# One thousand positions of a hand-ordered issue sequence, in another order

## The chip, the core and the metric

The kernel runs on one core of a Trainium2 chip. A core has five instruction queues that matter here: TensorE (PE) for matrix products, VectorE (DVE), ScalarE (ACT) and GpSimd (POOL) for everything element by element, and SyncE (SP), which here only issues DMA transfers. Each engine takes its instructions strictly in the order in which the program issued them to it, and waits at an instruction whose inputs are not there. The metric is the device time of one execution in microseconds (us).

## What is computed

Two layers. The first is an attention over 4 batches, 8 heads, 768 positions and 64 channels per head: every query sees the keys less than 16 positions away, and beside them one summary per block of 32 positions (the maximum of the block's keys, the mean of its values). The second is a feed-forward layer on the 3072 rows of 512 that come out.

```python
scores_s = scale * np.einsum('bhsd,bhnd->bhsn', q, k_sum)
scores_s = scores_s + np.log(block)
scores_l_m = np.where(mask_l, scores_l, -1000000000.0)
...
h = x @ w_in
g = np.maximum(h, 0.0) + np.log1p(np.exp(-np.abs(h)))
return (g @ w_out).astype(np.float32)
```

## The kernel before, in words

The rows are cut into six x tiles of 512 rows (two chunks of 256), numbered 0 to 5. For each x tile there are four attention **units**: two chunks times two halves of the heads (hp 0 and hp 2). A unit is a chain across the engines: PE makes the scores (line 644), DVE masks them and takes the row maxima (L657), ACT takes the exponentials (L665), DVE inverts the sums (L672, L673), one of POOL, DVE or ACT normalises (L678, L681), the result is transposed (for x tile 0 by PE at L698 with a copy by ACT at L702; for the others by DVE at L711, a store to memory and four reloads, L719 and L723), and PE multiplies by the values (L742). Of this product x is kept as two parts, a rounded high half and a low half with the rest (x tile 0: ACT L772 and DVE L776; later tiles: a copy at L754, then L828 and L835).

The feed-forward layer of an x tile goes over 16 feature tiles in two phases of 8. For each feature tile PE makes a hidden product in two halves of 6 products (L1060; the first half reads the columns of x that hp 0 makes, the second those of hp 2), ACT takes the softplus twice (L1162 rounded, L1166 exact), DVE keeps the rest (L1170), and PE projects (L1177): eight products with the rounded part, four with the rest. For the first and last feature tile of a phase the projection is four tasks, one per 128 rows.

The weights arrive as 64-bit words and are turned into two parts by a chain that is spread over the engines: magnitude (L934 on DVE or L937 on ACT), clamp (L941), shift (L945), sign (L949), tail (L955 on ACT, L958 on DVE), the addition of the tail on POOL (L963), the high part (L967) and the low part (L974).

None of this is scheduled at run time. The kernel first declares 2071 **tasks**, numbered in the order of declaration, each a handful of instructions with one or more ways to run it (one way per engine that could). Then `Order.issue` walks through the string `SEQUENCE` and runs the tasks in its order: a bare number takes the first way, a letter a or b the second or third. So the sequence fixes the order of every engine's queue at once, SP's included; the position of a task relative to tasks of other engines does not matter, only the order among those of its own engine. Buffers are fixed by the declaration, with the number of copies that the kernel gives them: one for the scores of a unit, one for the q, k and v of a unit of later tiles, two of PSUM for hidden products.

The tasks of which the prediction speaks: 0, 1, 2 the constants (identity, ones, mask); 3 to 42 products that fill PE's time; 43 to 49 key loads with their maxima; 51 to 62 value rows, loaded by SP and summed by PE, and 63 ACT's mean of them (L442); 64 to 135 the four units of x tile 0 (66, 101, 102, 106 are loads of value windows, 73 the first mask, 76 the first normalisation, 88 the second exponential, 117 and 131 the values products of the last two units, 119, 121, 133 and 135 their low halves); 136 to 139 copies of the means into the value sums by SP (L448); 153 to 245 the weights of the first phase (167, 172, 181, 188, 197, 201, 204 by name below; 180 and 208 are loads); 246 to 305 the feed-forward of x tile 0 (246 and 247 the first hidden product, 255 and 256 the second, 262 the third, 251 the first projection, 299 the rounded softplus of the eighth feature tile, 302 to 305 its projections); 312 to 440 the units of x tile 1 (313 and 342 key copies, 319 a copy of key maxima, 351 a mask, 352 the exponential behind it, 395 scores, 406 and 434 the values products of the last two units, 410 a low half of the third unit); 373 a key maximum; 386, 387, 589 key copies; 441 and 442 the first hidden product of x tile 1; 569 scores and 608 a values product of x tile 2.

The code as it is issued:

Of the kernel before, what the change touches and what calls it, by code (L numbers as in the profile page):

```python
# [147 lines left out]
0 3 4 5 6 7 8 9 10 11 12 13 14 153 154 2 43 162 15 16 17 18 19 20 21 22 23 24 25 26 27 28 1 29 30 31 32 33 313a 163a  # L148
155 156 157 158 189 164 45 165 167a 68 166 168 190a 152 44 46 64 51 191 192 193 169 159 53 100 55 319 57 314b 160 47
49 72 73 171 52 194 54 59 61 74 86 34 104 195 161 180 48 196a 87 66 172a 50 35 105 56 58 60 62 75 88 76a 63 312 108  # L150
197 65 67 173 109 70 170a 174 77 122 181a 78 175 182 107 89 79 36 37 69 208 38 176a 123 39 71a 40 110 90 111 80 322 81
41 112a 124 91 101 198 102 341 136 82 92 93 94 84 95 323 209a 137 347 177 342a 199 96 340 183 178a 125 368 210 184 213
98 179 97 185 85 83 113 138 99 106 324 211 114 186 204a 325 326a 372 115 350 42 103 116 227 126b 117 187a 369 127 200a
129 212 327 201 217 128 130 386 351 131 120 118 188a 387b 134 132 352 119 328 121 133 139 135 228 373 214 353 246 202
370 146 371a 140 385 247 248 374 249 250 376 203 255 392a 229 256 257 329 395 251 378 205 258 315 317 321 330 259 354b
355 262 320 396 263 143a 316 215 380 332 232 206 207 375a 218 318 331 414b 269 230 149 264 270 252 253 254 265 377
141a 260 271 356 272 397 266 219a 261 333 381 273 382 398 413 343 357 346 420a 267 360 216 220 415a 221 334 276 399b
336 231 359 379 345 423 348 358 223 222 277 344 400 349 507 508b 283 284 233 512a 424 224 268 236 401 278 279 509b 280
285 286 515 361 237 425 287 234a 235 388 383a 426 533 384 147 534a 274 362 402 389 290 535b 538a 238a 405 391 225 403
# [5 lines left out]
550 549 448 529a 537 464 574 598 449 455 459 700a 460 684 465 466 456 462 575 467 693 599 461 552 468 562 708 688a 576  # L165
600 471 601 530a 727 691 553a 567 565 472 563 478 473 602 709 694 479 578 463 557a 564 726 531 728a 532a 474 480 481
475 482 555a 710 469 579 733 577 470 363 692a 711 568 736 755 756b 580 485 712a 581 151 603 754 486 476 713 759 604
605 477 590 585 606 595 586 596 558a 492 593 335 583a 487 493 488 737 591 738 489 494 528 739 483 584 592 495 607 762
# [1181 lines left out]
```

## Time and profile before

| | us |
|---|---|
| median of 3 runs (lowest to highest) | 623.44 (622.63 to 623.88) |
| the profiled execution, its own time | 623.92 |
| its span, first to last instruction | 622.1 |
| PE busy | 599.2 |
| DVE busy | 389.8 |
| ACT busy | 349.6 |
| POOL busy | 180.7 |

The span is what the trace covers; the time of an execution also holds 1.8 us around it. Busy times are unions of the instructions' spans, so an engine at 96% has hardly a hole. In a timeline each line is a run of equal instructions on one engine, with its start, its length and, in brackets, how long the engine sat idle before it and whose result it waited for.

### The profile page before, as it was taken

The numbers are of one execution on the slowest core, as the hardware profiler recorded it, in microseconds if no ns is written. First come the engines' busy times: TensorE is split into PE (matmuls) and PEld (weight loads), VectorE is DVE, ScalarE is ACT, GpSimd is POOL, SyncE is SP. The second block draws the span as 40 slices with busy tenths as digits, with TensorE's granted clock in tenths as the row PEclk, the third lists the DMA queues.
The fourth block names the chain that finished last, engine by engine and source line by source line (L and its number), as shares of the span: only waits on it lengthen the run. The fifth ranks groups of instructions, "written<-read, shape, count | busy, mean of one in ns | idle before, by whom it ended". The sixth has DMA issues, their size and how long they took to land.

```text
span 622.1 us, 12000 instructions
## 1 busy us (share of the span) xinstructions
PE 599.2 (96%) x4452; PEld 506.4 (81%) x4452; DVE 389.8 (63%) x1010; ACT 349.6 (56%) x859; POOL 180.7 (29%) x180
## 2 busy tenths in 40 slices
PE   7668999999999999999999999999999999999997
PEld 6457777887888888888888888889898988989996
DVE  5989998676356755444316579873665664564532
ACT  4899999869567677565436987442312322132211
POOL 5444354041323213121000754474410325003000
PEclk9989999999999999999999999999999999999999
DMA  8986776976758677567435630023050240030031
GB/s 296 323 273 191 225 243 216 278 211 222 260 173 256 208 229 236 186 185 239 122 108 178 222 142 1 1 90 114 1 170 1 101 136 1 33 103 1 31 106 67
DMA packets 66571, 96.12 MB, mean 155 GB/s; under 512 B 5873, under 2 KB 44625, under 8 KB 65745
## 3 DMA queue, kind: packets, MB, share of 16 engines
q1 hardware_dynamic: 66512, 95.36, 48.0%
q8 instruction: 35, 0.57, 0.4%
q14 instruction: 24, 0.19, 0.1%
HBM read 66.06 MB, written 27.26 MB: 150 GB/s over the span
## 4 chain that ended last, share of the span: by engine, by line
PE 83%; DVE 7%; ACT 4%; DMA 2%; SPq 2%; issue 1%; ACTq 0%; DVEq 0%
PE po L1177 38%; PE ph L1060 21%; PE hx L1100 9%; PE hy L1100 7%; PE xo L742 4%; PE sc L644 3%; DVE sp L657 1%; DMA raw<-w_out_dram 1%; DVE t L941 1%; DVE w L974 1%; ACT t L937 1%; ACT sp L681 1%; DVE ks L353 1%; DMA v<-vs 1%; SPq L723 1%
## 5 line engine op out<-in xcount | busy, mean ns | idle before, releaser
L1177 PE MATMUL po<-w,gh 128*128 128x512 f32 x768 | 203.2, 392 | 0.1
L1177 PEld LDWEIGHTS po<-w,gh 128*128 128x128 f32 x768 | 141.1, 188 | 29.7 <-DVE ob L1207 0.7
L1060 PE MATMUL ph<-xw,w 128*128 128x512 f32 x672 | 161.2, 391 | 1.0 <-DVE xw L776 1.0
L1060 PEld LDWEIGHTS ph<-xw,w 128*128 128x128 f32 x672 | 125.6, 188 | 28.2 <-DVE xw L776 1.4
L1177 PE MATMUL po<-w,gl 128*128 128x512 f32 x384 | 114.3, 391 | 0.0
L1177 PEld LDWEIGHTS po<-w,gl 128*128 128x128 f32 x384 | 70.9, 188 | 14.4 <-issue 0.3
L665 ACT ACTIVATE sp<-sp,nm 128x120 f32<-128x120 f32 x192 | 73.1, 385 | 4.9 <-DVE nm L657 4.7
L1162 ACT ACTIVATE gh<-hx 128x512 fp32r<-128x512 f32 x20 | 12.0, 600 | 107.3 <-DVE hx L1110 107.3
L963 POOL TENSOR_TENSOR t<-t,raw 128x1024 int32<-128x1024 int32 (+1 forms) x20 | 41.9, 2101 | 94.3 <-DVE t L949 66.0
L1170 DVE TENSOR_TENSOR gl<-ph,gh 128x512 fp32r<-128x512 f32 x56 | 38.1, 685 | 44.7 <-ACT ph L1166 44.6
L1162 ACT ACTIVATE gh<-ph 128x512 fp32r<-128x512 f32 x56 | 33.3, 597 | 46.0 <-PE ph L1060 45.7
L804 POOL TENSOR_TENSOR x<-r,x 128x512 fp32r<-128x512 f32 x23 | 30.1, 1319 | 68.6 <-DVE x L797 58.9
L657 DVE CUSTOM_DVE_ANT_0 sp<-sc,added 128x120 f32<-128x120 f32 x192 | 40.9, 277 | 4.2 <-PE sc L644 3.3
L665 ACT ACTIVATION_READ_ACCUMULATOR sp<-sp,nm 128x1 f32 x192 | 36.5, 190 | 0.0
L1100 PE MATMUL hx<-x,w 128*128 128x256 f32 x240 | 35.7, 285 | 0.0
L1100 PE MATMUL hx<-x,sw 128*128 128x256 f32 x240 | 35.5, 284 | 0.0
L1100 PEld LDWEIGHTS hx<-x,w 128*128 128x128 f32 x240 | 32.9, 190 | 2.1
L1100 PE MATMUL hy<-x,sw 128*128 128x256 f32 x240 | 34.4, 284 | 0.0
L1162 ACT ACT_TABLE_LOAD x23 | 29.5, 1283 | 8.5 <-PE ph L1060 8.1
L1166 ACT ACTIVATE ph<-ph 128x512 f32<-128x512 f32 x56 | 33.0, 591 | 0.0
L1100 PEld LDWEIGHTS hx<-x,sw 128*128 128x128 f32 x240 | 32.0, 190 | 0.8
L1100 PEld LDWEIGHTS hy<-x,sw 128*128 128x128 f32 x240 | 31.2, 191 | 0.2
(113 smaller groups left out, 835.6 us busy)
## 6 DMA issues: line engine op xcount, KB each, us to landing
squares<-tb SPq DMA_DIRECT2D x20, 512.0 KB
pT<-squares SPq DMA_DIRECT2D x80, 128.0 KB
raw<-w_out_dram SPq DMA_DIRECT2D x16, 512.0 KB
kf<-kT_dram SPq DMA_DIRECT2D x16, 384.0 KB
raw<-w_in_dram SPq DMA_DIRECT2D x6, 1024.0 KB
q<-qT_dram SPq DMA_DIRECT2D x20, 256.0 KB
raw<-r SPq DMA_DIRECT2D x20, 256.0 KB
part<-ob SPq DMA_DIRECT2D x10, 512.0 KB
```

Of the source, the lines that this page charges most:

```text
L644: nc.tensor.matmul(unit(g * NU + h * NPAIR + i)[r * QW:(r + 1) * QW, k0:k1], lhsT=q[rows, w * QW:(w + 1) * QW], rhs=k[rows], start=True, s ...
L657: nc.vector.tensor_tensor_reduce(out=sp()[:, n], in0=unit(n), in1=added()[:, kinds.index((lows[w], lows[w + 1]))], scale=-SCALE, scalar=FL ...
L665: nc.scalar.activation(sp()[:, n], sp()[:, n], AF.Exp, bias=nm()[:, n:n + 1], scale=-1.0, accum_out=ss()[:, n:n + 1],)
L742: nc.tensor.matmul(xo()[h * D:(h + 1) * D, g * CH + w * QW:g * CH + (w + 1) * QW], lhsT=tiles.v(g)[:, w, h * D:(h + 1) * D], rhs=queries(g ...
L804: engine.tensor_tensor(to(1), a(), to(0).bitcast(F32), op=ALU.subtract)
L963: nc.gpsimd.tensor_tensor(a, a, word(0, I32), op=ALU.add)
L1060: nc.tensor.matmul(ph(), lhsT=lhs(part, cc), rhs=xw[cc][0]()[:, xw[cc][1], a], start=cc == 0 and n == 0, stop=cc == NCC - 1 and n == 2,)
L1100: nc.tensor.matmul(to()[:, half], lhsT=lhs(wa, cc), rhs=of_x(xa)[:, cc * CH:(cc + 1) * CH], start=cc == 0 and m == 0, stop=cc == NG - 1 an ...
L1162: nc.scalar.activation(gh(), all_of(), AF.Softplus)
L1166: nc.scalar.activation(all_of(), all_of(), AF.Softplus)
L1170: nc.vector.tensor_sub(out=gl(), in0=all_of(), in1=gh().bitcast(F32))
L1177: nc.tensor.matmul(po[t](), lhsT=a()[:, t * P:(t + 1) * P], rhs=w2()[:, part, i2 * DM:(i2 + 1) * DM], start=f == f0 and i == 0, stop=f == ...
```

## The change

The first 1000 positions of `SEQUENCE` are issued in another order; position 1001 and all that follow are as they were. The tasks, their buffers and what they depend on are the same. Of the tasks in these positions 109 run on another of their engines (their letter changes): among the larger ones, the first normalisation (76) goes from DVE to POOL and nine others change too; two low parts of weights go from POOL to DVE and one (197) from DVE to POOL; of the value sums of later batches four go from DVE to POOL and three the other way; eight copies of finished rows go from DVE to ACT and one back; eleven high halves of x go from DVE to ACT and five back; key copies are dealt out anew. On ACT the table of the exponential and that of the softplus replace each other 50 times over the whole program instead of 46, the first load counted in.

Places in single queues, counted from 0 within the queue: SP loads the value rows 59 and 61 at places 12 and 13 (before: 15 and 16), copies 136 and 138 at 23 and 24 (29 and 34), window 66 at 25 (19), 208 at 26 (25), 180 at 27 (18), 101, 102 and 106 at 28, 32 and 33 (26, 28 and 35). The reloads of the first unit of x tile 1 (329 to 332) stand at 49 to 52 (45, 50, 57, 54). On PE, 246 and 255 come at 61 and 65, before and just after the values product 131 at 64 (before: 64 and 66, with 131 at 63); the projections 302 to 305 all stand ahead of values 434 (before: 302 ahead, the other three behind). On POOL, the mask constants (2) come before the identity (0), and copy 589 comes ahead of the low half 410 (before: behind it).

The first 17 of the 36 lines, before and after:

```diff
-0 3 4 5 6 7 8 9 10 11 12 13 14 153 154 2 43 162 15 16 17 18 19 20 21 22 23 24 25 26 27 28 1 29 30 31 32 33 313a 163a
-155 156 157 158 189 164 45 165 167a 68 166 168 190a 152 44 46 64 51 191 192 193 169 159 53 100 55 319 57 314b 160 47
-49 72 73 171 52 194 54 59 61 74 86 34 104 195 161 180 48 196a 87 66 172a 50 35 105 56 58 60 62 75 88 76a 63 312 108
-197 65 67 173 109 70 170a 174 77 122 181a 78 175 182 107 89 79 36 37 69 208 38 176a 123 39 71a 40 110 90 111 80 322 81
-41 112a 124 91 101 198 102 341 136 82 92 93 94 84 95 323 209a 137 347 177 342a 199 96 340 183 178a 125 368 210 184 213
-98 179 97 185 85 83 113 138 99 106 324 211 114 186 204a 325 326a 372 115 350 42 103 116 227 126b 117 187a 369 127 200a
-129 212 327 201 217 128 130 386 351 131 120 118 188a 387b 134 132 352 119 328 121 133 139 135 228 373 214 353 246 202
-370 146 371a 140 385 247 248 374 249 250 376 203 255 392a 229 256 257 329 395 251 378 205 258 315 317 321 330 259 354b
-355 262 320 396 263 143a 316 215 380 332 232 206 207 375a 218 318 331 414b 269 230 149 264 270 252 253 254 265 377
-141a 260 271 356 272 397 266 219a 261 333 381 273 382 398 413 343 357 346 420a 267 360 216 220 415a 221 334 276 399b
-336 231 359 379 345 423 348 358 223 222 277 344 400 349 507 508b 283 284 233 512a 424 224 268 236 401 278 279 509b 280
-285 286 515 361 237 425 287 234a 235 388 383a 426 533 384 147 534a 274 362 402 389 290 535b 538a 238a 405 391 225 403
-291 427a 226a 239 428 390 393 394 404 516 297 298 292 275 293 541 294 406 240 299 241 338a 429 142 687 144 242 243 281
-430 407a 282 300 517 560b 301 364a 244a 431 432 518 519b 245 366 433 411a 566a 561b 416 288 422 289 520 412a 542 417
-418 543 295 296 302 419 408 421 559 434 150 337 569 409a 521 410a 435a 367 439 365 304 305 437 339a 510 306a 511 522
-524 544 588b 309a 310a 440a 438a 545b 303 525 441 442 587 443 594a 546 450 514 523 570 589 444 451 145 452 513 453 597
-571 148 445 307a 526 681 547 685 527a 536 454 689 446 572 540 699 548 682 447 686 457 573a 705 551 683 690 458 698 539
...
+2 43 153 162 189 45 64 68 51 44 0 1 3 53 158 154 4 155 5 156 6 157 7 8 9 163a 159 10 11 12 164 160 13 165 167 14 166
+15 161 55 47 190a 16 17 168 18 19 313b 20 46 21 314b 22 23 57 24 191 25 26 192 72 319a 194 193 59 52 61 73 195 74 54
+100 86 49 196a 65 104 56 171 87 197a 88 69 105 58 70 60 312 62 75 169a 76 48 27 63 107 28 29 30 67 50 136 31 32 33 34
+35 138 103 108 89 170a 66 90 208 36 109 37 180 38 110 39 40 77 101 172 122 173 315 320 174 176a 152 79 123 71a 78 41
+80 42 124 81 175 111 322 112a 91 340 341 347 323 102 93 84 106 82 177 92 209a 83 85 342 94 178a 95 210 211 324 125 113
+368 372 198 199 115 350 385 181 114 182 212 96 179 183 116 227 117 318 184 213 98 325 326a 97 126b 99 246 214 327 369
+120 127 185 118 129 373 186 128 130 131 351 386 392a 187 255 132 370 134 376 328 140 352 133 137 119 135 121 247 200
+317 380 201 202 374 387 395 256 188 203 248 228 249 257 371 250 258 251 139 329 331 215 330 332 262 204 353 259 263
+229 354b 230 316 231 269 321 270 264 355 396 205 265 232 217 218 252 356 253 271 378 272 254 233 206 260 381 266 273
+207 397 333 216 261 343 345 276 349 234a 334a 414 219a 398 277 375 377 357 360 399b 358 413 283 420 220 221 346 348
+143a 284 223 400 359 267 344 401 222 382 278 279 236 268 415 285 280 224 286 423 287 361 424 425 274 402 237 388 390
+391 235 290 405 379a 275 403 389 507 383a 362 508b 509 291 384 393 394 297 225 226 426 427a 292 293 238a 404 298 336
+364 239 281 240 242 512a 241 515 294 365a 428 243 406 533 516 429 282 517 416 422 288 534 538a 418 419 535a 244a 245
+421 417 289 518 146 407 541 299 409 338a 411 430 519a 295 433 432 520 431 300 559 296 301 304 305 141 303 560a 561b
+566 681 149a 542 685 302 543 142 521 337a 434 412a 339a 569 435a 587 588a 589 594a 437a 306 366a 510 514 438 367 439
+307 440 410a 441 442 544 545 511 450 522 524 443 523 444 150 525 513 451 309 445 144 310 546 446 452 453 447 547 689
+448 683 682 449 147 148 455 686 454 570 571 526 597 527a 531a 536 548 456 457 698 539 699a 572 705a 690 537 458 550
...
```

## Rows read from the trace of the kernel before

**Rows 1.** The page, busy time of each engine, its share and its instructions.
```profile
PE 599.2 (96%) x4452; PEld 506.4 (81%) x4452; DVE 389.8 (63%) x1010; ACT 349.6 (56%) x859; POOL 180.7 (29%) x180
```

**Rows 2.** Busy us (instructions) by stretch: sum of 10 to 60 us, then 60 to 110.
```profile
sum 50.00, PE 35.40 PEld 26.70 DVE 47.42 ACT 44.76 POOL 20.38; mean PE 7.08 PEld 5.34 DVE 9.48 ACT 8.95 POOL 4.08
...
60.00:110.00 50.00, 48.05 (x428) 38.72 (x427) 44.79 (x127) 47.80 (x138) 23.85 (x20) 1.00 0.75 230
```

**Rows 3.** PE's timeline: start, length, instruction, [idle before and its releaser].
```profile
45.66 1.97 PE L742 MATMUL xo<-pT,first 120*64 120x64 f32 x32 [4.93 <-ACT first L572]
...
54.21 4.15 PE L1060 MATMUL ph<-xw,w 128*128 128x512 f32 x17 [0.98 <-DVE xw L776]
...
59.26 0.74 PE L1177 MATMUL po<-w,gh 128*128 128x512 f32 x2
...
60.08 5.64 PE L1060 MATMUL ph<-xw,w 128*128 128x512 f32 x24
...
71.46 1.15 PE L742 MATMUL xo<-pT,v 120*64 120x64 f32 x32 [0.98 <-DVE gl L1170]
...
104.85 1.15 PE L742 MATMUL xo<-pT,v 120*64 120x64 f32 x32 [0.82 <-DMA v<-vs]
105.93 1.05 PE L644 MATMUL sc<-k,q 64*64 64x120 f32 x32
...
155.40 1.15 PE L742 MATMUL xo<-pT,v 120*64 120x64 f32 x32 [0.96 <-DMA st<-v_hp_dram]
```

**Rows 4.** DVE's timeline.
```profile
4.36 0.43 DVE L934 TENSOR_SCALAR t<-raw 128x512 uint32<-128x512 uint32 x1 [4.36 <-DMA raw<-w_in_dram]
...
12.46 1.59 DVE L941 TENSOR_SCALAR t<-t 128x1024 f32<-128x1024 f32 x1
...
19.03 0.94 DVE L353 TENSOR_REDUCE ks<-kf 128x24 f32<-128x768 f32 x1
...
23.62 1.16 DVE L678 TENSOR_TENSOR sp<-sp,ss 128x960 f32<-128x960 f32 x1
24.70 1.22 DVE L974 TENSOR_TENSOR w<-t,w 128x1024 fp32r<-128x1024 f32 x1
...
36.50 0.46 DVE L500 COPY k<-kf 128x288 f32<-128x288 f32 x2
...
38.94 0.69 DVE L941 TENSOR_SCALAR t<-t 128x1024 f32<-128x1024 f32 x1 [0.99 <-ACT t L937]
...
42.93 0.75 DVE L958 TENSOR_SCALAR raw<-raw 128x1024 int32<-128x1024 uint32 x1
...
53.08 1.41 DVE L776 TENSOR_TENSOR xw<-xo,xw 128x256 fp32r<-128x256 f32 x4
...
58.12 0.68 DVE L1170 TENSOR_TENSOR gl<-ph,gh 128x512 fp32r<-128x512 f32 x1
...
106.04 0.69 DVE L754 COPY r<-xo 128x512 f32<-128x512 f32 x1 [0.56 <-PE xo L742]
```

**Rows 5.** POOL's timeline.
```profile
12.22 1.27 POOL L963 TENSOR_TENSOR t<-t,raw 128x512 int32<-128x512 int32 x1
...
30.57 1.79 POOL L678 TENSOR_TENSOR sp<-sp,ss 128x960 f32<-128x960 f32 x1 [3.76 <-DVE ss L673]
...
90.13 2.40 POOL L974 TENSOR_TENSOR w<-t,w 128x1024 fp32r<-128x1024 f32 x1 [6.63 <-DMA v<-v_hp_dram]
...
107.25 1.65 POOL L835 TENSOR_TENSOR xw<-r,xw 128x256 fp32r<-128x256 f32 x2 [0.27 <-ACT xw L828]
```

**Rows 6.** ACT's timeline: the mean, then a table load and the first softplus.
```profile
24.39 0.59 ACT L442 ACTIVATE v<-vt 24x512 f32<-24x512 f32 x1
...
55.29 1.28 ACT L1162 ACT_TABLE_LOAD   x1
56.59 0.60 ACT L1162 ACTIVATE gh<-ph 128x512 fp32r<-128x512 f32 x1
```

**Rows 7.** SP's timeline: when a transfer is issued, and how long that took.
```profile
20.64 0.43 SPq L493 DMA_DIRECT2D q<-qT_dram  x1
```

More of the change, by code (lines that the diff above doesn't have):

```diff
@@ L168 @@
-605 477 590 585 606 595 586 596 558a 492 593 335 583a 487 493 488 737 591 738 489 494 528 739 483 584 592 495 607 762
-608 484 740b 490 491 695 556a 714 308 781a 496 498 785 715 696 609 611a 613a 612a 614a 782b 701 718 436 615 616 617
-780 741 703 311 763 618 497 499 716 697 500 501a 624 625 504a 930 502 764 619 702 620 742 707 717 631 765 766 788 610
-626 621 767 873b 622 934 632 627 628 638 789 879 872 704 639 874b 633 634 640 635 882 505a 641 706 901a 928 642 719
-623 629 768 902 743 790 791 645 646 729 732 931a 731 647 630 648 720 722 745 636 554 734 730 746 637 649 724a 744 735
@@ new lines @@
+566 681 149a 542 685 302 543 142 521 337a 434 412a 339a 569 435a 587 588a 589 594a 437a 306 366a 510 514 438 367 439
+307 440 410a 441 442 544 545 511 450 522 524 443 523 444 150 525 513 451 309 445 144 310 546 446 452 453 447 547 689
+448 683 682 449 147 148 455 686 454 570 571 526 597 527a 531a 536 548 456 457 698 539 699a 572 705a 690 537 458 550
+551 549 573 700 574 464 459 540 532a 460 461 598 575 684 693 145 599 687 462 465 708 726 600 601 552 562 567 576 579
+466 467 463 468 553 469 602 578 564 688 471 563 709 710 565 568 603 727a 694 733 728a 577 478 479 472 691 308 408 695
@@ new lines @@
+470 473 474 476 475 480 529 555 481 482 711 712b 736 580 604 755b 756a 485 713 605 754 590 596 581a 585 586a 486 607
+556a 335 591 692a 477 487 488 606 592 714 759a 489 930 151 696 492 737 738 595 493 483 593 484 739 762 740a 494 490
+780 741 742 495 311 781b 557 782b 496 785a 491 763 530 498 764 500 583a 584 608 609a 788 701 704 497 702 872 715 716
+613 697 873a 558 706 611a 612 717 436 501 502 614a 615 718 616 765 766a 624 617 703 618 625 707 879 767 619 620 621
+768 363 626 528 627 631 789 628 790 499 719 743 729 874a 928 882 720 632 791 901 907 900 744 746 735 745 504 505 792
@@ new lines @@
+622 734 730 623 932 731 633 629 793 634 931 635 630 883 884 638 902 732 936 503 645 794 639 885 646 722 640 641 642
+910 647 648 747 769 945 946 649 652 653 748 757 760 761 750 886a 887 751 771 770 724a 659 772 654 655 758 636 934 656
+888 506 637 660 773 795 796 661 662 643 774 778 783 752 776a 777 787 779 663 644 798 797 911 912 935a 929 933 650 786
+940 784 651 938 952a 913 666 947a 914a 667 955 915 956 799 974 975 657 753 800 875 877 876 889 939a 891 878 658 668
+804 669 664 892 916 670 723 725 957 665 674 673 672 880 554 775 973 582 890 881 958 802a 959a 941 942 803a 937 805a
@@ new lines @@
+806 815 807 980 816 808 809 810 671 817 818 893 675a 676a 678a 943 983 894 819 903 909 960 811 904 801 812 917 920 984
+985 986 822 961 1067 1068 908 1072 905 906 813 823 829 987 919 824 830 1069 988 679 814 831 820 825 832 826 833 1075
+1092b 896a 897a 918 921 1076 836 922 962 989 965 944 1096a 837 843 964 1091 948 950 954 951 949 1077 821 677 953 721
+827 828 834 1078 1079a 963 680 895 835 844 838 839 1093b 1099 840 845 846 966 924 1116 847 841 976 979 898 899 1117a
+990 992 977 610 1080 1081 1100 1122 1101 842 848 981 967a 850 851 852 982 857 971 926 972a 925a 858 968 1399 1115 993
@@ L184 @@
+853 849 969a 854 855 991 978 859 1102 994 860 995 1533 749 1125 1103a 1070 970 856 997a 1400 927a 999 861 1082 996
+1085 862 1071 1074 1084 1104 866 1000 998a 864 1142 1001 865 1002 1003 1141 1010 1073 1004 923 869a 1148a 870 1011
 1012 863 1083 1013 1105 1126 1143 1005 1014 1151 1086 1127 867a 1094 1006 1087 1007 1128 1089 1090 1097 1095 1401a
```

14 lines of the change are left out of this document (removed).

## The prediction, made before the change was run

> **What bounds the kernel now.** Read first the page's line of busy times: TensorE (PE) is busy 599.2 us of 622.1, so nearly everything is its queue [rows 1]. Then the busy table by stage: from 10 to 60 us PE works 35.40 us of 50, while VectorE (DVE) works 47.42 and ScalarE (ACT) 44.76; from 60 to 110 us PE has 48.05 of 50, with ACT (47.80) and DVE (44.79) nearly as full [rows 2]. So there are two regimes: a start in which DVE and ACT feed the first attention, then a stream of products in which PE hardly stops. The PE timeline shows the seam [rows 3]: a hole of 4.93 us before the values product at 45.66, one of 0.98 at 54.21 where the first feed-forward product waits for the last low half of x (DVE xw), 24 gapless products from 60.08, and after that only three waits of size, 0.98 at 71.46, 0.82 at 104.85 and 0.96 at 155.40, all before values products. The total work of PE is the same in both orders. What the change is worth is therefore how much earlier the stream begins, plus the three waits if they go, less the waits that the new order makes.
>
> **The start: DVE's queue.** The gate is task 135 and its neighbours, the four low halves of the fourth attention unit, which run from 53.08 [rows 4]. I counted the DVE tasks ahead of 135 in both orders: 60 before, 54 after. Gone from ahead of it are a normalisation (76, now on POOL; 1.16), a 1024-column low part of a weight (197, now on POOL; 1.22), a clamp (201; 0.69), a 1024-column tail (204; 0.75), a 512-column tail (167; no row kept, taken at the 0.43 of the same-sized magnitude), three small copies (313, 319, 342, at 0.46) and one low half of x (a quarter of 1.41, 0.35): 1.16 + 1.22 + 0.69 + 0.75 + 0.43 + 1.38 + 0.35 = 5.98. New ahead of it are two magnitudes (172, 181; 2 x 0.43) and one key maximum (373; 0.94): 1.80 [rows 4]. Net 4.2 us less on an engine that idles 2.6 us of those 50, so it counts nearly in full, if what feeds DVE comes earlier too. ACT has 41 tasks ahead of the exponential 352 in both orders, with three magnitudes gone and one tail and two small copies come: taken at nothing, as ACT idled 5.2 us of the 50 [rows 2], mostly for transfers.
>
> Against it stands POOL. In the stretch it takes 76, 197, 342 and 387 and gives up 188. A normalisation there is 1.79, a 1024-column low part 2.40, and a DVE clamp of 1024 columns took 1.59 beside a POOL addition at 12.22, where it is 0.69 elsewhere [rows 4, 5]. So some of POOL's new time comes back as longer DVE instructions. The bounds are 0 (none of the four meets such an instruction) and 4.2 (all of it held; one by one below). I take 1.0, one such meeting more than now, since the single row that shows a full meeting costs 0.90. The gate moves by 4.2 - 1.0 = 3.2.
>
> **From the gate to the stream.** Products 246 and 255 (the first halves of two hidden tiles, which read only what the first two attention units make) now stand ahead of the last low halves, so they fill holes; after the gate only 247, 395 and 256 are left ahead of 251. The product 251 needs the softplus of the first tile: exponential 352, then a table load (1.28 at 55.29), the two softplus passes and the DVE rest at 58.12, done at 58.80 [rows 4, 6]. 352 follows mask 351, which stands just ahead of the gate in both orders and moves with it. In the profile 251 began 0.46 after that, at 59.26, behind 395; with two products taken out of its way it can start at once. So 262, now at 60.08, starts 3.2 + 0.5 = 3.7 us sooner [rows 3]. Moving 0, 2 and 1 (mask constants ahead of the identity) only delays the filler products; mask 73 is the first reader of the constants and comes after 15 us either way. Cost nothing, covered by the first loads.
>
> **The stream.** The three waits before values products are read as transfers. For a1.0.0 the four reloads of the transposed scores stood apart in SyncE's (SP's) queue (places 45, 50, 54, 57), now at 49 to 52; between the values 406 and 434 there is now about one hidden half more of PE work; and 608 now comes behind four projections more. Each of these gives more time than its wait took, so I take all three off: 2.8, bounds 0 and 2.8. New: at the border to the second x tile, the four last projections 302 to 305 now come before values 434 instead of three of them behind it. Before, about 2.9 us passed from the end of these values to the last low half on POOL (take at 106.04, low halves to 108.90), and the scores at 105.93 and three projections covered it [rows 3 to 5]. Now only the scores (1.0) do; 441 needs 410, which on POOL stands behind copy 589, itself behind those scores. Bounds 0 and 1.9 (2.9 less 1.0); I take 1.4. For a new wait that I don't see I add one of the usual size, 0.9; bounds 0 and 2.8, three of them. Ahead of the softplus 299 ACT has one exponential and one table load more, but between the product it reads and the first use of its result stand six projections of whole tiles (281, 282, 288, 289, 295, 296), so nothing is charged.
>
> Sum: -3.7 - 2.8 + 1.4 + 0.9 = -4.2 us. The profiled execution took 623.92 (span 622.1 and 1.8 around it), 0.5 over the median of the runs. 623.9 - 4.2 = 619.7; the median should be at about **619.4**. About 0.2%, 1.2 us, is what a measurement of this kernel tells from no change.
>
> **Rivals.** *POOL holds DVE.* If every us that POOL gains ahead of the gate holds DVE for as long, 76 (1.79), 197 (2.40) and two copies (at least 0.46 each, as on DVE), less 188 (half of 2.40), are 3.9 us, and the gate moves only 0.3. Left are 0.5 by PE's order, the three waits and the new ones: -0.8 - 2.8 + 1.4 + 0.9 = -1.3, or 622.1 against the median; with one of the three waits kept it is 623. For it: the clamp of 1.59 [rows 4]. Against: that DVE worked 47.42 of 50 us beside 20.38 us of POOL without most of its instructions being longer [rows 2]. The page "SBUF — State Buffer" of the Trainium skill, section "SBUF: two separate sides", states such a lock: whichever of the two engines starts first keeps the shared port pair for its whole instruction, and the other blocks; the 1.59 agrees with it, and by it this rival would be the result wherever the DVE instruction is of the kind that takes the pair.
>
> *SP waits for the value sums.* This one ends slower. Copies 136 and 138 to the value sums now stand at SP's places 23 and 24 (they were at 29 and 34), ahead of the value windows 66, 101, 102, 106 and the weight loads 208 and 180. They wait for ACT's mean, which ended at 24.98 [rows 6]. SP was at the place before these, the load of q, at 20.64 [rows 7]. If the mean comes no sooner, SP stands still for 4.3 us, the windows for the third and fourth unit come up to 4.3 later, and values 117 and 131 wait for them: the gate then loses 4.3 where it would gain 3.2, +1.1; without PE's 0.5, with the waits before values kept, and with 1.4 + 0.9: +3.4, or 626.8. It decides if the mean ends later than about 23 us. I expect it near 22.5, since the last two value rows, 59 and 61, are loaded three places sooner (61 is SP's place 13, not 16) and exponential 88 no longer has a magnitude (172) ahead of it.
>
> *ACT gives the lead back.* Up to the second x tile the new order has two table loads more. If ACT, full from 60 to 110, is what PE waits for, it loses 2 x 1.28 there and, behind the extra exponential before 299, the lead of 3.7 shrinks to about 1: 622. The page "ScalarE: Activation LUTs" of the Trainium skill, section "What ACT_TABLE_LOAD costs", gives 1283 ns and a drain of about 1380 ns for each switch. The trace agrees on the load, but the next pass starts at 56.59, 0.02 after it [rows 6], so no drain is seen behind it; by the page's figure the loss would be 5.3 us, and this rival a slower one.
>
> **Chances.** The forecast 0.55; POOL holds DVE 0.13; ACT gives it back 0.13; SP waits, or another such loss over 1.2 us, 0.19. The forecast's own range: all bounds good (no POOL meeting, no new wait) is -4.7 - 2.8 = -7.5, or 615.9; with POOL's 1.0 doubled, no wait removed and 1.9 + 2.8 new it is +2; a likely worse end is 622. The 80% range is 615.5 to 625.5: it takes in the two middle rivals and leaves out most of the slow one. Faster by over 0.2%: forecast and a third of the middle rivals, 0.64; within: 0.16; slower: 0.20.
>
> **What would show it.** Right: low halves of the fourth unit done near 51 instead of 54.5, the first four-product run of 262 near 56.4, no wait over 0.5 before values of a1, and one of about 1.4 before the first product of the second x tile. Wrong: SP idle before the copies of the sums beyond 23 us; DVE clamps and shifts over 1.2 us in several places before 50; or PE's waits after 60 us adding up to more than 5 us.

## The result, and the profile after

The changed kernel took **632.61 us** (median of 4 runs, 631.47 to 633.33) beside 623.66 for the kernel before on the same chip (4 runs, 622.63 to 625.19): a ratio of 1.014, interval 1.0119 to 1.0161. The forecast was 619.4 and faster; it came out 9 us slower. The profiled execution took 632.57, its span is 630.8.

The page's busy times, beside [rows 1]:

```profile
PE 604.9 (96%) x4452; PEld 508.3 (81%) x4452; DVE 388.5 (62%) x1000; ACT 349.5 (55%) x838; POOL 185.8 (29%) x194
```

PE makes the same products, yet it is busy 5.7 us longer, since some of them ran at half the clock. The rest of the 8.7 us of span are 3 us more of idle time. The busy table by stage (us, instructions, then the granted clock; the first line is the sum of 10 to 60 us), beside [rows 2]:

```profile
sum 50.00, PE 40.56 PEld 30.83 DVE 44.33 ACT 43.49 POOL 24.74; mean PE 8.11 PEld 6.17 DVE 8.87 ACT 8.70 POOL 4.95
...
60.00:110.00 50.00, 47.48 (x353) 37.67 (x354) 46.26 (x119) 41.80 (x109) 21.50 (x20) 0.93 0.68 188
```

PE's timeline shows where: each line has its start, its length and, in brackets, the idle time before it and the releaser.

```profile
41.51 0.50 PE L1060 MATMUL ph<-xw,w 128*128 128x512 f32 x1
45.44 2.50 PE L1060 MATMUL ph<-xw,w 128*128 128x512 f32 x5 [3.44 <-DVE xw L776]
47.74 1.91 PE L698 MATMUL pt<-ident,sp 128*120 128x128 f32 x8
...
59.93 0.50 PE L1177 MATMUL po<-w,gl 128*128 128x512 f32 x1 [2.39 <-DVE gl L1170]
60.27 4.04 PE L1060 MATMUL ph<-xw,w 128*128 128x512 f32 x10
...
96.29 1.05 PE L644 MATMUL sc<-k,q 64*64 64x120 f32 x32 [1.51 <-ACT k L522]
98.24 1.02 PE L742 MATMUL xo<-pT,v 120*64 120x64 f32 x14 [0.90 <-DVE gl L1170]
...
115.18 1.21 PE L1060 MATMUL ph<-xw,w 128*128 128x512 f32 x4 [1.24 <-POOL xw L835]
...
139.70 2.11 PE L1177 MATMUL po<-w,gh 128*128 128x512 f32 x8 [0.81 <-ACT gh L1162]
...
148.91 1.43 PE L1177 MATMUL po<-w,gh 128*128 128x512 f32 x5 [0.74 <-ACT gh L1162]
...
167.41 0.50 PE L1177 MATMUL po<-w,gl 128*128 128x512 f32 x1 [0.64 <-DVE gl L1170]
...
195.31 1.15 PE L742 MATMUL xo<-pT,v 120*64 120x64 f32 x32 [0.75 <-DVE gl L1170]
```

The three waits of [rows 3] before values products are gone, and eight others have come behind 57 us. Read the first three lines together: one matmul of 246 goes, the other five wait 3.44 us, and the transpositions that stand behind them on PE go at 47.74, though their input was ready at 44.11 (ACT's first row below: 41.66 and 2.45). The hidden product 262 starts at 60.27, where it was 60.08: no lead at all. The timelines of DVE, POOL and ACT say why, in this order:

```profile
41.71 3.34 DVE L678 TENSOR_TENSOR sp<-sp,ss 128x960 f32<-128x960 f32 x1
44.98 0.74 DVE L776 TENSOR_TENSOR xw<-xo,xw 128x256 fp32r<-128x256 f32 x2
...
51.84 1.42 DVE L776 TENSOR_TENSOR xw<-xo,xw 128x256 fp32r<-128x256 f32 x4 [1.67 <-ACT xw L772]
...
55.84 2.31 DVE L949 SCALAR_TENSOR_TENSOR t<-raw,t 128x1024 uint32<-128x1024 uint32 x1
58.06 1.21 DVE L934 TENSOR_SCALAR t<-raw 128x1024 uint32<-128x1024 uint32 x1
59.20 0.68 DVE L1170 TENSOR_TENSOR gl<-ph,gh 128x512 fp32r<-128x512 f32 x1
```
```profile
41.65 2.39 POOL L963 TENSOR_TENSOR t<-t,raw 128x1024 int32<-128x1024 int32 x1 [6.17 <-ACT raw L955]
...
55.51 3.22 POOL L383 TENSOR_TENSOR st<-st 96x512 f32<-96x512 f32 x2 [7.37 <-PE sc L644]
```
```profile
41.66 2.45 ACT L681 ACTIVATE sp<-sp,ss 128x120 f32<-128x120 f32 x8
...
56.65 0.59 ACT L1166 ACTIVATE ph<-ph 128x512 f32<-128x512 f32 x1
```

A normalisation (326) that takes 1.16 elsewhere takes 3.34 beside POOL's addition, and the low halves that 246 needs come behind it. Later the rest pass 250 (59.20), which projection 251 waits for, stands behind sign 203 (2.31 beside POOL's value sum, 1.22 elsewhere) and magnitude 228; its own input was done at 57.24. The low halves of the fourth unit are done at 53.26, 1.2 earlier than before, not 3.2.

After two of these waits (2.39 at 59.93; 1.51 and 0.90 at 96 and 98) the clock falls. Here are two windows with the granted clock in the column after POOL's; 0.50 is the lower of the two levels, 1.2 GHz:

```profile
60.70:64.10 3.40, 3.40 (x9) 2.68 (x8) 3.33 (x4) 1.98 (x7) 2.02 (x1) 0.50 0.76 165
...
98.30:101.70 3.40, 3.40 (x36) 3.00 (x37) 3.26 (x19) 1.89 (x10) 3.40 (x4) 0.50 0.65 238
```

**Where the 8.7 us went.** From TensorE task 856 on both kernels issue the same products, 8.69 us later in the changed one (273.68 against 264.99), so all is lost before and nothing is won back. To place it, give each product its usual time at full clock and subtract the work done so far from the start of the next: this is an estimate of the time lost, by idling or by a slow clock, and it can be compared though the orders differ. (27 us of work is where 262 starts, 57 is at about 91 us, 222 at about 262.)

```
work done, us   27     36     57     66     78     96     114    150    222
before        32.44  32.48  34.25  34.69  35.90  36.24  36.66  38.50  40.06
after         32.63  34.35  35.51  40.06  41.85  43.26  44.65  47.33  48.75
difference     0.19   1.87   1.26   5.37   5.95   7.02   7.99   8.83   8.69
```

The head up to 262 gives and takes nothing (0.19); 1.7 is the slow clock behind the wait for 250; 0.6 is won back up to 57 us of work; 4.1 are the two waits at 96 and 98 with the slow clock behind them; 0.6 is the border to the second x tile; 2.9 more, up to 150 us of work, are the four waits of 139 to 195, 1.1 and 1.0 for the first two and 0.8 for the other two together.

### The profile page after: what moved, and what is told of

Same layout as the page of the kernel before. It is cut to its first block, busy times and chain, and to the rows that moved or that the text cites. A ratio compares the mean times of both kernels' runs of the same rounds, so it can differ in the third digit from the quotient of the medians.

```text
span 630.8 us, 11985 instructions
## 1 busy us (share of the span) xinstructions
PE 604.9 (96%) x4452; PEld 508.3 (81%) x4452; DVE 388.5 (62%) x1000; ACT 349.5 (55%) x838; POOL 185.8 (29%) x194
## 4 chain that ended last, share of the span: by engine, by line
PE 74%; ACT 13%; DVE 9%; DMA 1%; issue 1%; POOL 1%; SPq 0%; POOLq 0%; ACTq 0%; DVEq 0%
PE po L1177 36%; PE ph L1060 16%; PE hx L1100 9%; PE hy L1100 7%; ACT sp L665 4%; PE xo L742 3%; PE sc L644 2%; ACT L1162 2%; DMA kf<-kT_dram 1%; ACT L665 1%; DVE sp L657 1%; DVE gl L1170 1%; DVE t L941 1%; DVE t L949 1%; ACT gh L1162 1%
## 5 line engine op out<-in xcount | busy, mean ns | idle before, releaser
L1060 PE MATMUL ph<-xw,w 128*128 128x512 f32 x672 | 164.6, 396 | 4.8 <-DVE xw L776 3.4
L1060 PEld LDWEIGHTS ph<-xw,w 128*128 128x128 f32 x672 | 127.1, 191 | 33.5 <-DVE xw L776 3.8
```

Source lines behind the costliest of these rows:

```text
L1060: nc.tensor.matmul(ph(), lhsT=lhs(part, cc), rhs=xw[cc][0]()[:, xw[cc][1], a], start=cc == 0 and n == 0, stop=cc == NCC - 1 and n == 2,)
```

## Experiments

Every kernel has the same tasks; only places in the sequence differ, and against the changed kernel, in e4, e8, e10, e11, e13, e16, e17 and e18, the engines of some tasks. "Lag" is the start of task 856 against the kernel before (changed kernel: 8.69). It is taken from one profiled execution, and in e13 and e18 that one lay 1.4 and 2.0 us under its run's median; where lag and time disagree, the time counts. The expectations call ACT's softplus pairs (rounded, exact) GELU pairs, and the rest passes remainders.

More task numbers: 269 and 276 are hidden products of x tile 0, 333 a values product of x tile 1, 423 scores of x tile 1, 515 and 541 scores of x tile 2 with their key-sum copies 512 and 538. 259, 266, 273 and 294 are rest passes. Each is the last to read a PSUM bank, a buffer that products are written to; the next product that gets this bank waits for the pass. 469 and 476 are projections of x tile 1 behind the softplus pairs 466, 467 and 473, 474; 471 and 485 are hidden products of x tile 1.

| run | us | ratio to before, interval | lag |
|---|---|---|---|
| e1 rest first | 631.77 | 1.0087 to 1.0140 | 6.50 |
| e2 no jump | 631.39 | 1.0092 to 1.0128 | 6.60 |
| e3 key copy | 632.89 | 1.0110 to 1.0153 | 8.94 |
| e4 new head | 627.60 | 1.0029 to 1.0067 | 3.43 |
| e5 both covers | 632.70 | 1.0108 to 1.0159 | 8.31 |
| e6 head fixed | 629.98 | 1.0061 to 1.0128 | 6.07 |
| e7 all fixed | 628.46 | 1.0045 to 1.0089 | 4.26 |
| e8 old head | 631.64 | 1.0091 to 1.0143 | 7.95 |
| e9 all waits | 642.70 | 1.0288 to 1.0319 | 19.00 |
| e10 order alone | 657.96 | 1.0523 to 1.0579 | 32.29 |
| e11 engines alone | 637.83 | 1.0181 to 1.0264 | 13.76 |
| e12 late waits | 647.20 | 1.0353 to 1.0388 | 24.05 |
| e13 fixed head, old rest | 624.64 | 1.0007 to 1.0033 | -0.84 |
| e14 projections first | 635.46 | 1.0142 to 1.0212 | 11.01 |
| e15 late projections | 633.39 | 1.0137 to 1.0183 | 9.14 |
| e16 bank wait | 624.59 | 1.0003 to 1.0026 | -0.05 |
| e17 lead kept | 625.24 | 1.0019 to 1.0043 | 1.29 |
| e18 next wait | 627.29 | 1.0025 to 1.0054 | 1.23 |

### The head: e1, e2, e6

```diff
-DVE: 203 228 250            (e1)
+DVE: 250 203 228
-PE:  246 127 129 131        (e2; e6 is both)
+PE:  127 129 131 246
```

> The new order with two weight tasks, 203 (sign, 2.31 us in its profile) and 228 (magnitude, 1.21), issued right behind the first softplus rest 250 instead of ahead of it on DVE. Theory (the first projection 251 waits because 250 stands behind these two, and the idle PE is then granted half its clock from 60.7 to 64.1 us): the wait of 2.39 us in 251 shrinks below 0.5, no half clock appears near 60 to 64, and 262 starts about 2 us sooner, near 58.2; with the 1.6 us of the half clock the whole is 3 to 3.6 us shorter than the new order. Rival (251 is late with the whole last attention unit, so that rest 250 has its inputs only near 59): 262 moves by less than 0.5 and the time by less than 1.

> The new order with hidden half 246 issued behind the values product 131 instead of ahead of transposes 127 and 129 on PE. Theory (246 waits on PE for DVE's low halves and holds up the last unit behind it): the transposes of the last unit start near 44.5 instead of 47.74, its low halves are done near 50.5 instead of 53.3, and 262 starts 2 to 3 us sooner. Rival (these low halves are bound by DVE's queue, whatever PE does): the transposes come sooner but the low halves stay within 0.7 of 53.3 and the time within 1 us of the new order.

> The first two experiments at once: signs 203 and magnitude 228 behind remainder 250 on VectorE, and hidden product 246 behind values product 131 on TensorE. Alone they gave 0.8 and 1.2 us in time, and each took 2.1 to 2.2 off the lag of projection 856 (8.69 to 6.50 and 6.60). Theory (each takes away another link of one chain: 246's place delays the transpositions, 203's place the remainder 250, and hidden product 262 waits for both): 262 starts at 56.4 to 57.5, no half clock before 65, but the next wait in front of values product 333 eats part of it as in the first experiment: lag of 856 5 to 6, 629 to 630 us. Rival A (they add in full): lag 4.4, 628.2. Rival B (both are held by the same end of the low halves at 53, so the second adds nothing): lag 6.5, 631.3.

e1 brought 262 from 60.27 to 58.05, e2 to 59.15, both together to 56.69, so 3.4 us before [rows 3] and within 0.3 of the forecast's 56.4. PE's timeline of e6:

```profile
56.36 0.50 PE L1178 MATMUL po<-w,gl 128*128 128x512 f32 x1 [0.56 <-DVE gl L1171]
56.69 5.65 PE L1061 MATMUL ph<-xw,w 128*128 128x512 f32 x24
...
68.05 1.15 PE L743 MATMUL xo<-pT,v 120*64 120x64 f32 x32 [1.85 <-DVE gl L1171]
```

So the forecast's chain is right but for two misplaced tasks. But of the 3.6 us of lead over the changed kernel only 2.6 are left at task 856: the last line shows part of it going in a wait for a PSUM bank, which a DVE rest pass frees. By itself each move gave less than expected: e1's lag fell by 2.2 where 3 to 3.6 were expected (a wait of 1.98 before 333 came in), and in e2 the last low half is done at 52.1, not 50.5. In time, e1, e2 and e6 are not clear of the changed kernel, whose interval (1.0119 to 1.0161) theirs overlap.

### Which half holds the loss: e4, e8

```diff
+e4: first 247 positions of the changed sequence, then the order and engines of before
+e8: first 248 positions of before, then the changed order and engines
```

> The first 247 positions of the new order (up to the first projection 251), then all other tasks in the order and on the engines of the kernel before. Theory (the head costs about 0.2 us until 262 and 1.6 by the half clock behind it, the other 7 us come from what follows): 1 to 3 us slower than before. Rival (the head makes the whole loss, since its late tasks leave ACT and DVE behind for long): 6 us or more slower than before.

> The other half of e4: the order of before with its engines up to the first projection 251 (248 positions), then the changed order and engines. Theory (the head gives 2 to 3 us of the loss, the half clock behind it included, and the waits at 96, 98, 115, 139, 148, 167 and 195 stand by themselves): 629.5 to 631. Rival (the waits behind 90 us come from the late head, as the transfers and sums of the next batch of values start behind it): 625 or less.

The new head alone costs 3.4, a little more than expected, the new rest alone 7.9 (its head, in the order of before, was 2.3 late at 262 in this execution, with the clock down for 17 us of the start instead of 10; from there on it loses 5.6). The waits at 97, 99, 114, 139, 148, 166 and 194 stand in e8 at the sizes they have in the changed kernel, so they come with the new rest. As e8's head was late too, that they don't need a late head is shown by e6: there 262 is 3.6 us sooner than in the changed kernel, and they stand at 1.10, 0.92, 1.23, 0.81, 0.76, 0.62 and 0.75.

### The waits at 96 and 98, and the border: e3, e5, e7

```diff
-ACT: 225 292 293 238 ... 242 512     (e3, e5, e7)
+ACT: 512 225 292 293 238 ... 242
-DVE: 239 240 241 294                 (e5, e7)
+DVE: 294 239 240 241
-POOL: 589 410                        (e7, with the moves of e6)
+POOL: 410 589
```

> The new order with the small copy 512 (key maxima for the first unit of x tile 2) issued on ACT nine places sooner, ahead of weight task 225. Theory (scores 515, which wait 1.51 us for it at 96.29, are only the first to meet a stall that values 406 would have too, since its last loads are issued at 92.34): the wait before 515 goes, the one before 406 grows to about 2.4, 406 still starts near 98, and the time stays within 0.7 us of the new order. Rival (the copy itself costs the time): 406 starts 1.5 sooner, no half clock near 98, and the whole is 1.5 to 3.2 us shorter.

> Two moves in the changed order around 90 to 98 us: VectorE's remainder pass 294 (ready at 91.93 by its two ScalarE passes, but started at 97.50 behind the weight passes 239, 240, 241) stands ahead of 239, and ScalarE's key-sum copy 512 stands ahead of the weight pass 225. Moving 512 alone gave nothing, since products 406 then waited 2.74 for 294 alone. Theory (the two waits 1.51 and 0.90 lie over each other, and the half clock of 98.3 to 101.7 behind them costs some 1.7 more, so only both moves together take it away): idle before 515 and 406 under 0.5 together, no half clock there, and the projection 856 some 4 us ahead of the changed kernel's: about 628.5 us. Rival (the weight passes of the fourth group, now later, hold the next projections instead, so the time moves and is not won): 631 to 632.5.

> The moves of e5 and e6 together, and ScalarE's and VectorE's share left as the change has it, with GpSimd's key copy 589 moved behind low half 410 (the 1.24 wait at the border, before hidden product 441). Theory (the loss is a sum of a few places where one queue's order puts work ahead of what TensorE waits for): 8.7 - 3 (e6) - 4 (e5) - 1 (589) leaves 0 to 2 us over the time before: 624 to 626. Rival (the engines as a whole are too full in the changed split of the 109 tasks, so each mended wait comes back elsewhere): 628 or more.

In the changed kernel DVE ran rest pass 294 at 97.50, behind three weight passes, though its input was done at 91.93. With 512 alone moved, 406 took the whole wait (2.74 at 97.74), as expected, though it waited for 294 and not for a load. With both moved, both waits went, and a third took their place, 2.23 before scores 541, for a key-sum copy that ACT has behind an exponential; PE's timeline of e5:

```profile
94.79 1.05 PE L645 MATMUL sc<-k,q 64*64 64x120 f32 x32
95.77 1.15 PE L743 MATMUL xo<-pT,v 120*64 120x64 f32 x32
...
102.98 1.05 PE L645 MATMUL sc<-k,q 64*64 64x120 f32 x32 [2.23 <-ACT k L523]
```

So e5 won nothing (lag 8.31), as its rival had it, though by another task than the weight passes that the rival named. In e7 the moves together gave 4.4 of the 8.7 us, short of the 624 to 626 expected and within its rival (628 or more): the border's 1.24 is gone, the wait before 541 is 1.76.

### Carrying on: e9, e12, e14, e15

```diff
-ACT: 599 466 467, 710 473 474, 738 494 495, 884 640 641 647 648   (e9 on top of e7, e12 alone)
+ACT: 466 467 599, 473 474 710, 494 495 738, 640 641 647 648 884
-PE:  333 261 ... 267, 469 471, 476 736, 498 500 608, 747 636          (e14 on top of e7; e15 last four alone)
+PE:  261 267 333, 471 469, 736 476, 608 498 500, 636 747
```

e9 also moves 266, 538, 300, 301 and 534 forward; e9 and e12 put hidden product 639 ahead of 645 on PE and the rests 496 and 642 forward on DVE; e14 puts 541 behind 295.

> On top of e7 the waits that e7 still shows: VectorE's remainder 266 ahead of transposition 355 and mask 396 (wait 1.97 before values product 333, with a half clock behind it, 1.7); ScalarE's key-sum copy 538 ahead of exponentials 517 (1.76 before scores 541); exact copy 300 and remainder 301 earlier (0.5); exponentials 599 and 710 behind the GELU pairs 466/467 and 473/474 (0.81, 0.75), 738 behind 494/495 (0.64), hidden product 639 ahead of 645 and exponentials 884 behind 648 (0.75). Theory (every loss is a place in one queue's order, and the split of the 109 tasks over the engines is not the limit): the lag of projection 856 falls from 4.26 to -4 if all of it comes, -1 if half: 620 to 625, so level with the time before or under it. Rival (engines too full, waits come back): 627.5 or more.

> The changed kernel with the moves behind 130 us alone: exponentials 599 behind 466/467, 710 behind 473/474, 738 behind 494/495 with remainder 496 ahead, hidden product 639 ahead of 645, exponentials 884 behind 648. Theory (waits 0.81, 0.74, 0.64 and 0.75 stand by themselves, with some 0.3 of slower issue at each: the loss table shows 1.0 to 1.2 at each): lag of 856 8.69 to about 5.5 (4.2 taken off at most), 629 to 630.5. Rival (exponentials later by 3 to 7 us hold the transposed probabilities and so the values products behind them): 632 or more.

> On top of e7 only TensorE's order, no other queue: projections 261 and 267, ready for long, stand ahead of values product 333 (wait 1.97 for a bank); scores 541 behind projection 295 (1.76); projection 469 behind hidden product 471 (0.81), 476 behind scores 736 (0.75), values product 608 ahead of projections 498 and 500 (0.64), projection 636 ahead of values product 747 (0.75). Theory (TensorE has ready work behind each of these waits, so they fill; the half clock of 68.5 to 71.9 goes too): lag of 856 from 4.26 to between 0 and 2, 624 to 626. Rival (as in e9, VectorE's weight halves and norms end when they end, and TensorE waits for them one task later): 627.5 or more.

> The changed kernel with the four late moves of e14 alone (469 behind 471, 476 behind 736, 608 ahead of 498, 636 ahead of 747). Theory (these four waits are TensorE's own order and nothing else, 1.0 to 1.2 each in the loss table): lag of 856 from 8.69 to 4.5 to 6.5, 628.3 to 630.5. Rival (behind each stands the same late ScalarE pair, so the wait only moves by one task): 632 or more.

All four times came out as the rivals had them. e12 traded waits of 0.6 to 0.8 for these on PE:

```profile
142.94 5.74 PE L1061 MATMUL ph<-xw,w 128*128 128x512 f32 x24 [1.64 <-DVE gl L1171]
...
159.35 1.22 PE L1061 MATMUL ph<-xw,w 128*128 128x512 f32 x2 [4.48 <-DVE gl L1171]
...
208.87 3.35 PE L1061 MATMUL ph<-xw,w 128*128 128x512 f32 x7 [4.03 <-ACT r L755]
```

An exponential that is put off holds the tasks behind it on ACT (copy 748, behind the last of them, frees the bank at 208.87). e15's one move that mattered shows the small form: with 471 ahead of 469 the wait of 0.81 for the softplus becomes one of 2.03 for a bank (PE, 140.53), since 471 needs the bank that the same pair and its rest pass free. So in these places neither putting off ACT's exponentials nor another order on PE helps; that the waits are ACT's and DVE's pace is the reading that is left, and no run lightens those two queues to test it. In e9 the wait before 333 went and one of 1.86 for a weight half (DVE, L975) came 3 us after it.

### Order and engines apart: e10, e11

```diff
+e10: the changed order, every task on its engine of before
+e11: the order of before, the 109 tasks on their new engines
```

> The changed order, but each of the 109 tasks on its engine of before. Theory (the order puts work ahead of what TensorE waits for): 629 to 634, with the waits before 262, 515, 469 and 476 still there. Rival (it is the 109 moves: meetings of VectorE and GpSimd, ScalarE's two more table loads): 626 or less.

> The order of before, with the 109 tasks on the engines that the change gives them. Theory (the order does the harm, the engines little by themselves; some moved tasks come at places of the order that were made for another engine): 623 to 627. Rival (the moves do the harm): 629 or more.

Both are much worse than the changed kernel itself (by 25 and 5 us), and than expected (629 to 634 and 623 to 627), so neither can be named the cause: order and engines fit each other, and the two losses don't add up to the 9 us. e11 does say that the moves aren't harmless in another order, as its rival had it.

### Is the lead worth anything: e13, e16, e17, e18

```diff
+e13: the head of e6 (247 positions), then the order and engines of before
-DVE: 204 353 229 259                          (e16 on e13)
+DVE: 259 204 353 229
-ACT: 215 232 206 414 264 265                  (e17 on e16)
+ACT: 264 265 215 232 206 414
+e17: 266 right behind 396, 216 ahead of 375 (DVE), 507 right behind 423 (SP)
+e18 on e17: 273 ahead of 375, 230, 377 and 141 (DVE)
```

> The changed order up to 251 (247 positions) with the two moves of e6 in it (246 behind 131; 203 and 228 behind 250), then the order and engines of before. Theory (the forecast's chain of head, gate and hidden products is right but for these two places, and before's rest keeps a lead, giving back what its own waits at 71 and 105 don't hide): 262 at 56.5 to 57 against 60.1, lead at 856 of 0.5 to 3.5, 620.5 to 623.5. Rival (e4's other losses behind 262, 1.56 before the values products and 1.09 before scores 515, come whatever the head's time is, or grow, since transfers and value sums were placed for the old head): lag 0 or more, 624 to 627.

> e13 with one more move on VectorE: remainder 259 (ready at 57.36 by its ScalarE passes, but run at 61.67, behind the inverse 353 and the clamp 229 that took 2.80 beside GpSimd's addition) right behind 258, so ahead of 204, 353 and 229. It frees the bank that hidden product 269 waited 2.75 for. Theory (the lead of 3.3 at 262 lives on to the next wait, before values product 333, where remainder 266 still runs at 70 and takes 2 to 3 of it back): wait before 269 gone, lead at 856 of 0.5 to 2, 621.5 to 624. Rival (the whole lead is lost at 333, and the inverse, now later, holds the mask of 396): 624 or more.

> e16 and three more: ScalarE's pair 264, 265 ahead of the weight passes 215, 232, 206 and VectorE's remainder 266 right behind mask 396 (frees the bank for values product 333); VectorE's weight half 216 ahead of value sum 375 (for hidden product 276); SyncE's query load 507 right behind scores 423 that free its buffer (1.05 before scores 515). Theory (a lead is kept only where every wait behind it moves forward as well, and these four are the next ones): lead at 856 of 1.5 to 3, 620.5 to 622.5, so faster than before. Rival (weights, value sums and the following exponentials are as late as before, and the lead ends in waits for them, as in e9): 624 or more.

> e17 with remainder 273 (ready at 67.99, run at 73.36) right behind its ScalarE pass 272, ahead of value sum 375, shift 230, key maximum 377 and running total 141 on VectorE: the bank for hidden product 276, which waited 3.33. Theory now (between 57 and 75 VectorE is busy for 17.7 of 18 us and ScalarE for 14.6 to 17.5, so a lead of TensorE at 262 is a lead on work that these two have to supply and ends at the next thing that they deliver): the wait before 276 shrinks or goes, but a wait for weights, sums or queries within the next 15 us takes its place; lag at 856 within 1.5 of before's, 623 to 625.5. Rival (each of these waits was one misplaced task, and this was the last before a free stretch): lead at 856 of 2 or more, 621.8 or less.

This is the forecast's head as it was meant, ahead of a rest whose own waits are known. 262 starts 3.31 us earlier in e13 than in the kernel before. PE's timelines of e13, e16, e17 and e18 at the place where the lead ends:

```profile
62.40 3.02 PE L1061 MATMUL ph<-xw,w 128*128 128x512 f32 x12 [2.75 <-DVE gl L1171]
```
```profile
71.30 1.98 PE L743 MATMUL xo<-pT,v 120*64 120x64 f32 x32 [4.35 <-DVE gl L1171]
```
```profile
74.09 2.50 PE L1061 MATMUL ph<-xw,w 128*128 128x512 f32 x5 [3.33 <-DVE gl L1171]
```
```profile
77.09 1.79 PE L645 MATMUL sc<-k,q 64*64 64x120 f32 x32 [4.81 <-ACT sp L682]
```

Each mended wait carries the lead some tasks further, to 3.7 at 276 in e18, and the next wait takes nearly all of it: product 269 starts only 0.4 ahead of its time of before (e13), then 333 only 0.2 (e16), then 276 only 0.4 (e17), and scores 423 are 1.1 late (e18). A long wait also brought the half clock in e16, e17 and e18, and so a loss. In time e13, e16 and e17 came out as their rivals had them, and e18 (627.29) slower than both its theory and its rival had it. The busy columns of 57 to 75 us, before and in e18 (PE, PEld, DVE, ACT, POOL):

```profile
57.00:75.00 18.00, 17.02 (x129) 13.56 (x129) 16.93 (x42) 17.52 (x48) 6.83 (x6) 1.00 0.76 223
```
```profile
57.00:75.00 18.00, 15.19 (x92) 12.13 (x92) 17.68 (x42) 14.00 (x38) 6.81 (x6) 1.00 0.61 155
```

VectorE is busy for 94% of this stretch before, and for 98% in e13, e16, e17 and e18 alike, while ScalarE falls from 17.52 to 14.00 us in e18. So the lead is a lead on what VectorE above all has still to deliver. This is read from the busy times; no run takes work off VectorE to show it. No version here beats the kernel before; e13 and e16 come within 0.2%.

## Why the prediction was wrong, point by point

- **"Products 246 and 255 ... stand ahead of the last low halves, so they fill holes": wrong.** A product fills a hole only if its input is there before the hole begins. 246's low halves came at 45.4 and 45.7, and on an in-order queue it held the two transpositions behind it. e2 shows its price: 262 comes 1.1 sooner, and the lag falls by 2.1.
- **"With two products taken out of its way it can start at once" (251): wrong.** The step looked at PE's queue and not at DVE's, where 203 and 228 now stand ahead of rest 250. e1: 262 comes 2.2 earlier.
- **POOL's 1.0 and the gate's 3.2: near in sum, mis-sized in their parts.** One meeting, norm 326, cost 3.34 - 1.16 = 2.2 ahead of the gate, and sign 203 lost another 2.31 - 1.22 = 1.1 behind it. The norm began 0.06 after POOL's addition and ended at 45.05, 1.0 after the addition's end at 44.04: it was held for nearly the whole of it. The page "SBUF — State Buffer" of the Trainium skill, section "SBUF: two separate sides", states this lock; the trace agrees, and by that rule the meeting should have been priced by POOL's instruction (2.4) and not by the 0.90 of one row. The rival that POOL holds DVE had the mechanism for part of the gate's loss. But the forecast also overlooked a meeting that the change takes away: clamp 201, counted as 0.69, took 1.80 before, beside an addition of POOL (DVE and POOL before):

```profile
49.74 1.80 DVE L941 TENSOR_SCALAR t<-t 128x1024 f32<-128x1024 f32 x1
```
```profile
48.58 2.40 POOL L963 TENSOR_TENSOR t<-t,raw 128x1024 int32<-128x1024 int32 x1 [1.16 <-DVE t L949]
```

  One meeting of 2.2 more and one of 1.1 less make 1.1, beside the 1.0 taken: that is luck. In e6, with 246 out of the way, the last low half is done at 51.41, 3.1 earlier than before, where 3.2 was forecast. The list of DVE's tasks leaves out two small ones, 187 (gone, 0.42) and 169 (new, 0.38), which cancel.
- **"262 ... starts 3.7 us sooner": wrong in the kernel as it stands (it was 0.2 later), right as a chain,** since with the two tasks mended it is 2.7 to 3.5 sooner (3.4 in e6). **The deeper step that failed is that a lead at 262 is worth its length.** [Rows 2] gave ACT 47.80 and DVE 44.79 of 50 us, and the prediction read PE as the bound there because it was at 48.05. With three engines that full, a lead of one ended at the next thing that another delivered: e13, e16, e17 and e18 saw that four times. The rival that ACT gives the lead back named it, for one exponential; it priced it at 622, where e13, with the lead whole at 262, took 624.6.
- **The three waits before values products went, but one was misread.** In the loss table they show as 0.6 between 36 and 57 us of work and little later, since others came in the same stretches. The forecast read all three as transfers. Its own row at 71.46 names a DVE rest pass ([rows 3], gl): 333 waits for a bank. This is the very wait that comes back at 1.98 in e1, 1.85 in e6 and 4.35 in e16, and it was not the reloads that ended it. Of the signs that the forecast set, "no wait over 0.5 before values of a1" failed at 406 (0.90).
- **Right: the border.** 1.4 was forecast before 441, for POOL's low half behind copy 589; it is 1.24, and e7 took it away.
- **"For a new wait that I don't see I add one of the usual size" (0.9): mis-sized.** Six came, 1.51, 0.90, 0.81, 0.74, 0.64 and 0.75, together 5.4, and the slow clock behind the first two. With the border's 1.24 that is 6.6 after 60 us, over the 5 that the forecast set as a sign of being wrong.
- **ACT's two more table loads, charged at nothing: right at 299, but the look ended there.** In the changed kernel PE waits for no result of 299. The softplus passes that PE waits for at 139.70 and 148.91 each stand behind a load, as on ACT here:

```profile
137.75 1.28 ACT L1162 ACT_TABLE_LOAD   x1
139.05 0.60 ACT L1162 ACTIVATE gh<-ph 128x512 fp32r<-128x512 f32 x1
```

  The pass starts 0.02 after the load, as in [rows 6], so a switch costs its 1.28. In the kernel before, the first of the two passes had no load ahead of it (126.96); the second had one (134.74), but PE came to its projection only at 146.04. That the added loads make the two waits is not shown: e12, with 48 loads instead of 50, is slower.
- **SP: nearly right.** The mean ended at 23.04 (ACT, 22.45 and 0.59 long), 0.5 later than expected and just where the slower rival was to decide; SP went on at 23.06, after 2.5 us idle and not 4.3. The values product 117, which that rival had late, started at 40.42, before [rows 3]. The result is slower for other reasons than that rival.

What stays open is why the changed rest loses 5.6 us more than that of before even behind the head of before (e8). Its waits are known one by one, and mending the head and those up to the border gave half of the 8.7 us (e7). But those behind 130 us went only where larger ones came, and the split into order and engines doesn't separate them.

## What to carry to other kernels

Before a lead is counted as time, look at every engine that supplies the stretch behind it: where two or three are nearly full (94 to 97% here), the lead ended at the first result that one of them delivered on its own schedule, and a wait of about two us or more could cost clock as well. In an in-order queue a task moved forward is a gain only if its input is ready at its new place, which is to be asked of each queue on the way (here DVE for a PE product). A mended wait is worth what the next one leaves of it, so mend them together, or measure how far the gain travels. And take from a row who ended a wait before naming its cause.

## What the runs showed of the chip that was not expected

- **Long waits in mid-stream cost clock, but not every one.** A wait of 2.39 at 59.93 was followed by 3.4 us at half clock, and so cost an estimated 1.7 more; so did 2.74 in e3, 4.35 in e16 and 4.81 in e18, and 3.33 in e17 was followed by 6.8 us. In e13 a wait of 2.75 at 62.40 was followed by full clock to the end of the stream. Nor does the length of the wait tell which: one of 1.85 in e6 (68.05) was followed by half clock, one of 2.23 in e5 (102.98) was not.
- **A VectorE instruction beside a GpSimd one can take three to four times as long:** normalisation 3.34 for 1.16, clamp 2.80 for 0.69. The second is from DVE's and POOL's timelines of e13:

```profile
58.95 2.80 DVE L942 TENSOR_SCALAR t<-t 128x1024 f32<-128x1024 f32 x1
```
```profile
58.79 2.41 POOL L964 TENSOR_TENSOR t<-t,raw 128x1024 int32<-128x1024 int32 x1 [2.37 <-DVE ss L673]
```

- **Putting off four exponentials behind one or two softplus pairs cost 15 us** (e12 against the changed kernel, one hidden product and two rests moved with them), five times the 2.9 us of waits that it was to save.
